# Reordering the factor stage of the first batch: forward factor first, its own banks for the way back, transposes four steps ahead

## Chip, cores, metric

The kernel runs on one core of a Trainium2 chip. The metric is device time in microseconds (us) of one execution; lower is better.

## What is computed

A global filter along the sequence (real FFT, multiplication by a complex filter, inverse real FFT), followed by a feed-forward layer with ELU, all in float32:

```python
# x: (8, 3008, 256); filt_r, filt_i: (1505, 256); w_in: (256, 2048); w_out: (2048, 256)
X = np.fft.rfft(x, axis=1)
Y = X * (filt_r + 1j * filt_i)[None]
y = np.fft.irfft(Y, n=3008, axis=1).astype(np.float32)
h = y.reshape(24064, 256) @ w_in
g = np.where(h > 0, h, np.exp(np.minimum(h, 0)) - 1)
out = g @ w_out
```

The inputs arrive as float64 where the kernel reads the two weights, and it turns their bit patterns into float32 itself.

## The kernel before

**The filter.** The length 3008 is split as 47 times 64. For each of the 8 batches the sequence goes through four matmul stages with tables: a 64-point stage (`a_first` for batch 0, `a_unit` for the others), a 47-point forward factor (`b_unit`), after the multiplication by the filter the 47-point way back (`bi_unit`), and the last 64-point stage (`n_unit`). Between `bi_unit` and `n_unit` the data is turned over through DRAM: `y_write` (L333) stores, `y_read` (L344) loads it in the other order.

The middle stages work on 8 groups, g = 0 to 7 (`NG`). For one group of batch 0:

- `t_first(g)` (L260) transposes with TensorE (PE): eight 112x128 transposes (L269) into two PSUM banks of the pool `psO` (names po0 to po3; group g takes po0 and po1, or po2 and po3, by its parity), which ScalarE (ACT) copies to an SBUF tile t2 in two halves (L270). Tiles of groups 2 and 3 come from the pool `t4p`, all others from `t2p`, two buffers each.
- `b_unit(0, g)` (L299) is the forward factor: four 64x512 products (L297) into two banks, psr and psi. VectorE (DVE) then makes four products with the filter tile ff (L309 to L312): sr, si, and sp, sq (for even g) or the two tiles pq (for odd g). sr and si have two buffers in the pool `sp`.
- `bi_unit(0, g)` (L322) is the way back: eight 64x512 products (L297) from those four tiles into two banks, pva and pvb, which ACT copies to t3 (L329, L330; two buffers).
- `y_write(0, g)` issues two DMAs of 192 KB on SyncE's queue (SP); of the last group one of the two on ACT's.

psr, psi, pva and pvb come from one rotating list of four PSUM banks, `banks` (pool `psM`), so that each pair taken waits for the readers of the pair before the last.

**The weights.** w_in and w_out are read in 16 pieces, k = 0 to 15. `w_fetch(k)` (L546) issues the DMA, `w_split(k)` (L571, DVE, two instructions) masks mantissa and exponent, `w_float(k)` (L579, ACT, four instructions, L584 to L593) makes floats of them, `w_join(k)` (L595, DVE) multiplies them together and for odd k adds the four sums of the fast matrix product (L620 to L623). Even and odd pieces have a set of scratch tiles each. Pieces 7 to 11 are decoded beside the middle stages of batch 0, and pieces 12 to 14 right behind them, as fill work for DVE and ACT.

**The order.** It is written out by hand (`tc.manual_schedule()`): each engine runs its instructions strictly in the order of the program, and semaphores make it wait for what it needs. The order around the change is the loop at L713. It runs ten steps; step g holds group g's forward factor and group g-2's way back, ahead of them the transposes of group g+2 (those of groups 0 to 3 are done before the loop). After the loop come `w_float(12)`, the reading `y_read(0, 0)` (four DMAs of 128 KB, in turn from SP and from ACT), more decoding, the first loads of batch 1, and `n_unit(0, 0)`.

**The main part.** After that a plan mixes the filter stages of batches 1 to 7 into the feed-forward products of the batch before (`up_steps`, `down_steps`, a seven-product scheme for 2x2 blocks), 192 quads in all. This part is not touched.

Of the kernel before, what the change touches and what calls it, by code (L numbers as in the profile page):

```python
# [11 lines left out]
FP32 = mybir.dt.float32  # L12
# [14 lines left out]
P = 128  # L27
D = 256
# [6 lines left out]
NG = K2 // 4  # L35
# [78 lines left out]
def kernel(  # L114
# [25 lines left out]
    t2p = pool("t2p", 2)  # L140
# [3 lines left out]
    t4p = pool("t4p", 2)  # L144
# [4 lines left out]
    psO = pool("psO", 1, space=PSUM)  # L149
# [20 lines left out]
    def bank(name, shape=(P, 2, D)):  # L170
        i = banks.pop(0)
        return i, psM.tile(list(shape), FP32, tag="m%d" % i, name=name)
# [86 lines left out]

    def t_first(g):  # L260

        t = t2s[0, g] = (t4p if g in (2, 3) else t2p).tile([P, 4, D], FP32, tag="t4" if g in (2, 3) else "t2", name="t2")
        for j in range(2):
            i = 2 * (g % 2) + j
            ps = psO.tile([P, 2, 256], FP32, name="po%d" % i)
            for u in range(2):
                k = 4 * g + 2 * j + u
                for dh in range(2):
                    nc.tensor.transpose(ps[0:ROWS, u, ts(dh, P)], zt[k // 16][dh][:, ts(k % 16, ROWS)], eye)  # L269
            nc.scalar.activation(out=t[0:ROWS, 2 * j:2 * j + 2, :], in_=ps[0:ROWS], func=AXT.Copy)  # L270
# [23 lines left out]
    def tile_mm(ps, table, k, rhs, special):  # L294
        for u, w, v in ((0, 1, 1), (1, 1, 0)) if special else ((0, 2, 0),):
            for n, r in enumerate(rhs):
                nc.tensor.matmul(ps[:, u:u + w, :], table[k, v, :], r[k, u:u + w, :], start=n == 0, stop=n == len(rhs) - 1)  # L297

    def b_unit(b, g, f=None, gb=gb, pq=None):  # L299
        t = t2s.pop((b, g))  # L300
        f = fbufs[(b * NG + g) % FBUFS] if f is None else f
        (i0, re), (i1, im) = (bank(n) for n in ("psr", "psi"))
        for o, a in ((0, 0), (64, 2)):
            for ps, k in ((re, LO), (im, HI)):
                tile_mm(ps[o:o + 64], gb, k, [t[:, a:a + 2, :]], g == 0 and a == 0)
        sr, si = (sp.tile([P, 2, D], FP32, tag=n, name=n) for n in ("sr", "si"))
        p, q = pq or (qp.tile([P, 2, D], FP32, tag=n, name=n) for n in ("sp", "sq"))

        nc.vector.tensor_tensor(out=sr, in0=re, in1=f[:, 0], op=ALU.mult)  # L309
        nc.vector.tensor_tensor(out=si, in0=re, in1=f[:, 1], op=ALU.mult)  # L310
        nc.vector.scalar_tensor_tensor(out=p, in0=im, scalar=-1.0, in1=f[:, 1], op0=ALU.mult, op1=ALU.mult)  # L311
        nc.vector.tensor_tensor(out=q, in0=im, in1=f[:, 0], op=ALU.mult)  # L312
        banks.extend((i0, i1))
        if b == 0:

            ss[b, g] = [sr, p], [si, q]
            return
        nc.gpsimd.tensor_tensor(out=sr, in0=sr, in1=p, op=ALU.add)  # L318
        nc.gpsimd.tensor_tensor(out=si, in0=si, in1=q, op=ALU.add)
        ss[b, g] = [sr], [si]  # L320

    def bi_unit(b, g):  # L322
        s = ss.pop((b, g))
        t = t3s[b, g] = t3p.tile([P, 4, D], FP32, tag="t3", name="t3")
        (i0, pa), (i1, pb) = (bank(n) for n in ("pva", "pvb"))
        for o, table, sv in ((0, gr, s[0]), (64, gi, s[1])):
            for ps, k in ((pa, LO), (pb, HI)):
                tile_mm(ps[o:o + 64], table, k, sv, g == 0 and k == LO)
        nc.scalar.activation(out=t[:, 0:2, :], in_=pa, func=AXT.Copy)  # L329
        nc.scalar.activation(out=t[:, 2:4, :], in_=pb, func=AXT.Copy)  # L330
        banks.extend((i0, i1))

    def y_write(b, g, queues=(nc.sync, nc.sync)):  # L333
        if g == 0:
# [236 lines left out]
    def w_split(k):  # L571
        m, e, c = wtmp[k % 2 if k < 15 else 0]
        f, l = c[:, 0], c[:, 1]
        wts[k] = m, e, f, l
        hi = wds[k][:, :, 1]
        nc.vector.tensor_scalar(out=m, in0=hi, scalar1=0x000FFFFF, scalar2=None, op0=ALU.bitwise_and)
        nc.vector.tensor_scalar(out=e, in0=hi, scalar1=0x7FF00000, scalar2=None, op0=ALU.bitwise_and)

    def w_float(k, part=None):  # L579
        m, e, f, l = wts[k]  # L580
        if part == 1:
            return w_power(e)

        nc.scalar.activation(out=l, in_=wds[k][:, :, 0], func=AXT.Identity, scale=2.0 ** -52)  # L584
        nc.scalar.activation(out=f, in_=m, func=AXT.Identity, scale=2.0 ** -20, bias=1.0)
        if part is None:
            w_power(e)
# [56 lines left out]
    with tc.manual_schedule():  # L644


        with tc.tile_pool(name="boot", bufs=1) as bp:
            ff = bp.tile([P, NG, 2, 2, D], FP32, name="ff")
            once = bp.tile([P, 2, P], FP32, name="once")
            eye, gf = once[:, 0], once[:, 1].rearrange("p (v q) -> p v q", v=2)  # L650
            pq = [bp.tile([P, 2, D], FP32, name="pq%d" % i) for i in range(2)]
            zt[0] += [bp.tile([P, 16 * ROWS], FP32, name="zt%d" % i) for i in range(2)]

            for z in zt[0] + zt[1]:
                nc.gpsimd.memset(z.rearrange("p (k r) -> p k r", r=ROWS)[:, :, 48:64], 0.0)
            for k in (1, 2, 3):
                w_fetch(k)
            f_arrange()
            w_fetch(0, nc.sync)
            for c in range(NXC):  # L660
                x_place_first(c)
            for c in range(3):
                x_load_first(c)
            w_fetch(4, nc.sync)
            nc.scalar.memzero(ff[:, 0:NG // 2])
            nc.vector.memset(ff[:, NG // 2:NG], 0.0)
            wtmp.append([kp.tile([P, 512], U32, tag=t, name=n) for t, n in (("k0", "wm"), ("k1", "we"))] +
                        [kp.tile([P, 2, 512], FP32, tag="c", name="wfl")])
            wtmp.append([sdp.tile([P, 2, D], FP32, tag="sd", name=n).bitcast(U32).rearrange("p a b -> p (a b)")
                         for n in ("wm", "we")] +  # L670
                        [t1p.tile([P, XC, D], FP32, tag="t1", name="wfl").rearrange("p (a b) d -> p a (b d)", a=2)])
            for i, v in enumerate((1151.0 * 2 ** 23, 255.0 * 2 ** 23)):
                nc.vector.memset(edges[:, i:i + 1], v)

            def step(k):
                w_split(k)
                w_float(k)
                if k > 0:
                    w_join(k - 1)

            for k in range(3):
                step(k)
            w_fetch(5, nc.sync)
            for c in (3, 4):
                x_load_first(c)
            a_first(0)
            w_fetch(6, nc.sync)
            x_load_first(5)
            nc.sync.dma_start(once, once_d)
            nc.sync.dma_start(gs, gs_d)  # L690
            step(3)
            for c in (1, 2):
                a_first(c)
                w_fetch(c + 6, nc.sync)
            step(4)
            a_first(3)
            w_fetch(9, nc.sync)
            step(5)
            step(6)
            for c in (4, 5):  # L700
                a_first(c)
            tn_read(0, 0)
            for g in range(NG):
                f_read(0, g, ff[:, g])
                if 3 <= g < 5:
                    w_fetch(g + 7)
            for k in (12, 13, 14):
                w_fetch(k)
            w_split(7)
            w_join(6)  # L710
            for g in range(4):
                t_first(g)
            for g in range(NG + 2):  # L713
                if 2 <= g < NG - 2:
                    t_first(g + 2)
                if g >= 2:
                    bi_unit(0, g - 2)
                if g < 5:
                    w_float(g + 7)
                if g < NG:  # L720
                    b_unit(0, g, ff[:, g], gf, pq if g % 2 else None)
                if g >= 2:
                    y_write(0, g - 2, (nc.sync, nc.scalar if g == NG + 1 else nc.sync))
                if g < 4:
                    w_join(g + 7)
                    w_split(g + 8)
                if g == 7:
                    w_join(11)
                    w_split(12)
                    w_split(13)  # L730
            w_float(12)
            y_read(0, 0, (nc.sync, nc.scalar))
            w_float(13)
            w_join(12)
            w_fetch(15)
            w_split(14)
            w_join(13)
            w_float(14)
        for c in range(2):
            x_load(1, c)  # L740
        yp = pool("yp", 2)
# [105 lines left out]
```

## Time and profile before

| | |
|---|---|
| median of 4 runs | 2647.75 us (2646.73 to 2647.93) |
| the profiled execution's own time | 2647.9 us |
| its span, first to last instruction | 2646.1 us |
| granted TensorE clock, mean over the span | 0.993 |
| PE busy, 0 to 44 us | 18.89 us |
| PE busy, 44 to 97 us (the stage of the change) | 41.53 us |
| DVE busy, 44 to 97 us | 39.13 us |
| ACT busy, 44 to 97 us | 32.25 us |
| PE busy, 97 to 120 us | 16.73 us |
| PE busy, 120 to 2646 us | 2517.82 us |

The profile is taken from one execution; its times run from the first instruction. It gives for every instruction its start, duration, source line, and the idle time of its engine just before, with what ended that idle time. "PE" is a matmul, "PEld" the loading of its weights, "SPq" or "ACTq" the issue of a DMA on that engine's queue. A busy PE can run at half speed; the granted clock says so (1.00 is full speed). A float32 matmul shows as several records, and matmuls on different quarters of the array overlap, so that durations of records add up to more than the time that passes.

### The profile page before, as it was taken

How to read it: one execution, taken by the hardware profiler on the slowest of the kernel's cores; microseconds unless marked ns; L12 is line 12 of the kernel's file. 1: busy time of each engine (PE TensorE's matmuls, PEld its weight loads, DVE VectorE, ACT ScalarE, POOL GpSimd, SP SyncE). 2: the span in 40 equal slices, each digit the busy share in tenths (PEclk: the TensorE clock that was granted, in tenths of full speed). 3: DMA queues.
4: the chain of work that ended last, by engine and by line, in shares of the span. 5: the costliest groups of instructions: out<-in, count | busy, mean ns of one | idle time of the engine just before them, and what ended most of it. 6: DMA issues, size and time to landing. Idle time of an engine off the chain costs nothing.

```text
span 2646.1 us, 37334 instructions
## 1 busy us (share of the span) xinstructions
PE 2595.0 (98%) x13508; PEld 2210.0 (84%) x13508; DVE 1843.9 (70%) x3203; ACT 1508.2 (57%) x2622; POOL 237.1 (9%) x298
## 2 busy tenths in 40 slices
PE   5799999999999999999999999999999999999998
PEld 4588789887898878988789878898789887899887
DVE  6777767677676776667767676666767677666766
ACT  6565555555555555655556555565555555555554
POOL 5001100012000210002100020001200011000000
PEclk8899999999999999999999999999999999999999
DMA  9534312523133331423213341134321333110010
GB/s 293 134 95 106 86 38 55 126 73 84 39 97 87 80 78 43 103 69 101 72 31 98 85 113 49 39 90 107 98 50 41 79 81 82 38 41 19 21 29 17
DMA packets 224456, 202.85 MB, mean 77 GB/s; under 512 B 127586, under 2 KB 191090, under 8 KB 224272
## 3 DMA queue, kind: packets, MB, share of 16 engines
q1 hardware_dynamic: 211632, 166.70, 25.0%
q0 software_dynamic: 11184, 33.04, 4.8%
q8 instruction: 107, 1.75, 0.3%
q10 hardware_dynamic: 1456, 0.72, 0.1%
q14 instruction: 77, 0.63, 0.1%
HBM read 128.52 MB, written 74.97 MB: 77 GB/s over the span
## 4 chain that ended last, share of the span: by engine, by line
PE 96%; DMA 2%; DVE 1%; POOL 0%; issue 0%; ACT 0%; DVEq 0%; SPq 0%; POOLq 0%; ACTq 0%
PE po L490 43%; PE phs L408 25%; PE phd L408 12%; PE pha L408 6%; PE psn L360 3%; PE pva L297 2%; PE psr L297 2%; PE psa L209 2%; DMA fd<-in_filt_i_dram 1%; DMA ff<-fd 0%; DMA wd<-in_moe_w_out_dram 0%; DMA fd<-in_filt_r_dram 0%; PE pvb L297 0%; DMA yd<-t 0%; PE psi L297 0%
## 5 line engine op out<-in xcount | busy, mean ns | idle before, releaser
L490 PE MATMUL po<-g,wo 128*128 128x256 f32 (+1 forms) x5376 | 1296.7, 375 | 0.0
L490 PEld LDWEIGHTS po<-g,wo 128*128 128x128 f32 x5376 | 1015.0, 190 | 129.5 <-issue 15.8
L419 ACT ACTIVATE g<-phs 128x512 f32<-128x512 f32 (+1 forms) x576 | 338.9, 588 | 842.8 <-PE phs L408 842.2
L416 DVE TENSOR_TENSOR g<-phd,g 128x512 f32<-128x512 f32 (+1 forms) x384 | 259.6, 676 | 457.2 <-ACT e L426 282.3
L426 ACT ACTIVATE e<-e 128x512 f32<-128x512 f32 (+1 forms) x768 | 477.1, 621 | 24.4
L408 PE MATMUL phs<-y,wi 128*128 128x256 f32 (+1 forms) x1536 | 394.8, 379 | 0.0
L408 PE MATMUL phs<-ys,wi 128*128 128x256 f32 (+1 forms) x1536 | 387.6, 375 | 0.7 <-ACT g L419 0.6
L430 DVE SCALAR_TENSOR_TENSOR g<-e,g 128x512 f32<-128x512 f32 (+1 forms) x576 | 387.2, 672 | 0.0
L425 ACT ACTIVATE e<-g 128x512 f32<-128x512 f32 (+1 forms) x576 | 353.0, 613 | 32.6 <-DVE g L416 27.4
L408 PEld LDWEIGHTS phs<-y,wi 128*128 128x128 f32 x1536 | 284.5, 190 | 83.1 <-ACT t L329 34.1
L408 PEld LDWEIGHTS phs<-ys,wi 128*128 128x128 f32 x1536 | 291.4, 190 | 34.5 <-ACT g L419 1.4
L430 DVE SCALAR_TENSOR_TENSOR g<-e,phs 128x512 f32<-128x512 f32 (+1 forms) x192 | 130.0, 677 | 136.9 <-ACT e L426 136.7
L408 PE MATMUL phd<-ys,wi 128*128 128x256 f32 (+1 forms) x768 | 194.1, 375 | 1.2 <-DVE g L416 1.2
L408 PE MATMUL pha<-y,wi 128*128 128x256 f32 (+1 forms) x768 | 193.8, 375 | 0.0
L408 PE MATMUL phd<-y,wi 128*128 128x256 f32 (+1 forms) x768 | 193.7, 375 | 0.0
L425 ACT ACTIVATE e<-phs 128x512 f32<-128x512 f32 (+1 forms) x192 | 113.0, 588 | 141.4 <-PE phs L408 140.5
L318 POOL TENSOR_TENSOR sr<-sr,sp 128x512 f32<-128x512 f32 x56 | 71.1, 1270 | 1246.6 <-DVE sp L311 1246.6
L408 PEld LDWEIGHTS phd<-ys,wi 128*128 128x128 f32 x768 | 145.5, 190 | 18.6 <-DVE g L416 2.3
L408 PEld LDWEIGHTS pha<-y,wi 128*128 128x128 f32 x768 | 145.8, 190 | 16.8 <-ACT y L362 0.2
L408 PEld LDWEIGHTS phd<-y,wi 128*128 128x128 f32 x768 | 145.8, 190 | 16.5
L467 DVE TENSOR_TENSOR g<-g,g 128x512 f32<-128x512 f32 (+1 forms) x192 | 130.7, 681 | 6.7
L470 DVE TENSOR_TENSOR g<-g,g 128x512 f32<-128x512 f32 (+1 forms) x192 | 130.7, 681 | 6.6
(133 smaller groups left out, 2372.0 us busy)
## 6 DMA issues: line engine op xcount, KB each, us to landing
yd<-t SPq DMA_DIRECT2D x127, 192.0 KB
t<-yd SPq DMA_DIRECT2D x190, 128.0 KB
z<-t SPq DMA_DIRECT2D x84, 256.0 KB
f<-fd POOLq DMA_DIRECT2D x112, 192.0 KB, 3.6
t<-z SPq DMA_DIRECT2D x224, 96.0 KB
out_dram<-o SPq DMA_DIRECT2D x632, 32.0 KB
tn<-tn_t SPq DMA_DIRECT2D x48, 256.0 KB
xc<-in_x_dram SPq DMA_DIRECT2D x84, 128.0 KB
```

The lines of the kernel that those rows point to most:

```text
L297: nc.tensor.matmul(ps[:, u:u + w, :], table[k, v, :], r[k, u:u + w, :], start=n == 0, stop=n == len(rhs) - 1)
L318: nc.gpsimd.tensor_tensor(out=sr, in0=sr, in1=p, op=ALU.add)
L360: nc.tensor.matmul(ps[:, ts(q, P)], t[:, i - 4 * m, ds(dh * P, P)], w[:, i - 4 * m, :], start=True, stop=True)
L408: nc.tensor.matmul(ps[:, a, 0:h], w_in[q][:, COMBO[n], a, :], y[n], start=start and a == 0, stop=True, skip_group_check=True)
L416: nc.vector.tensor_tensor(out=g[o], in0=i0, in1=i1, op=ALU.add)
L419: nc.scalar.activation(out=g[o], in_=i0, func=AXT.Copy)
L425: nc.scalar.activation(out=e, in_=src, func=AXT.Relu, scale=-1.0)
L426: nc.scalar.activation(out=e, in_=e, func=AXT.Exp, scale=-1.0)
L430: nc.vector.scalar_tensor_tensor(out=g[n], in0=es[n], scalar=1.0, in1=src, op0=ALU.subtract, op1=ALU.max)
L467: nc.vector.tensor_tensor(out=b12, in0=b22, in1=b12, op=ALU.subtract)
L470: nc.vector.tensor_tensor(out=g["t4"], in0=g["b21"], in1=g["t2"], op=ALU.subtract)
L490: nc.tensor.matmul(po[i][:, u, 0:h], w_out[q][:, COMBO[n], a, :], g[n][:, a, :], start=q == 0 and a == 0 and n in (1, 3, 6, 4), stop=True, ...
```

## The change

The change touches the first batch's middle stages alone.

- In each step the forward factor's products of group g come first, then the way back of group g-2 (called between those products and the four multiplies, through the new argument `between`), then the transposes of group g+4. Before, the order was transposes of g+2, way back, forward factor.
- The rotating list of four banks is left to the forward factor. The way back of batch 0 takes its banks from `psO`: po2 and po3 for groups 0 to 2, then po0 and po1 for odd and po2 and po3 for even groups.
- Transposes of groups 4 to 7 all go through po0 and po1. Their SBUF tiles are taken from `t4p` for groups 2, 3, 6 and 7.
- Fill work: `w_float(g+7)` now follows the transposes in step g. `w_join` and `w_split` run in steps 0 to 2 instead of 0 to 3; piece 11 is split in step 2, and piece 10 is joined in step 7, ahead of piece 11. After the loop `w_float(14)` stands before `w_join(13)`, which leaves the order on each engine as it was.

```diff
     def t_first(g):
-        t = t2s[0, g] = (t4p if g in (2, 3) else t2p).tile([P, 4, D], FP32, tag="t4" if g in (2, 3) else "t2", name="t2")
+        pool, tag = (t4p, "t4") if g % 4 > 1 else (t2p, "t2")
+        t = t2s[0, g] = pool.tile([P, 4, D], FP32, tag=tag, name="t2")
         for j in range(2):
-            i = 2 * (g % 2) + j
-            ps = psO.tile([P, 2, 256], FP32, name="po%d" % i)
+            i = j + 2 * (g % 2 if g < 4 else 0)
+            ps = psO.tile([P, 2, 256], FP32, tag="po%d" % i, name="po%d" % i)
...
-    def b_unit(b, g, f=None, gb=gb, pq=None):
+    def b_unit(b, g, f=None, gb=gb, pq=None, between=None):
...
                 tile_mm(ps[o:o + 64], gb, k, [t[:, a:a + 2, :]], g == 0 and a == 0)
+        if between:
+            between()
...
     def bi_unit(b, g):
...
-        (i0, pa), (i1, pb) = (bank(n) for n in ("pva", "pvb"))
+        if b == 0:
+            pa, pb = (psO.tile([P, 2, 256], FP32, tag="po%d" % i, name="po%d" % i)
+                      for i in ((0, 1) if g > 2 and g % 2 else (2, 3)))
+        else:
+            (i0, pa), (i1, pb) = (bank(n) for n in ("pva", "pvb"))
...
-        banks.extend((i0, i1))
+        if b > 0:
+            banks.extend((i0, i1))
...
             for g in range(NG + 2):
-                if 2 <= g < NG - 2:
-                    t_first(g + 2)
-                if g >= 2:
-                    bi_unit(0, g - 2)
+                back = (lambda g=g: bi_unit(0, g - 2)) if g >= 2 else None
+                if g < NG:
+                    b_unit(0, g, ff[:, g], gf, pq if g % 2 else None, back)
+                else:
+                    back()
+                if g < 4:
+                    t_first(g + 4)
                 if g < 5:
                     w_float(g + 7)
-                if g < NG:
-                    b_unit(0, g, ff[:, g], gf, pq if g % 2 else None)
+                if g < 3:
+                    w_join(g + 7)
+                    w_split(g + 8)
+                if g == 2:
+                    w_split(11)
                 if g >= 2:
                     y_write(0, g - 2, (nc.sync, nc.scalar if g == NG + 1 else nc.sync))
-                if g < 4:
-                    w_join(g + 7)
-                    w_split(g + 8)
                 if g == 7:
+                    w_join(10)
                     w_join(11)
                     w_split(12)
                     w_split(13)
...
             w_split(14)
+            w_float(14)
             w_join(13)
-            w_float(14)
```

## The prediction

> **What bounds the kernel now.** I read the page first, its second part: TensorE (PE) is saturated from about 116 us to the end, and only the first two of the 40 slices have room.
>
> ```profile
> span 2646.1 us, 37334 instructions
> PE   5799999999999999999999999999999999999998
> PEclk8899999999999999999999999999999999999999
> ```
>
> So whatever this change gains or loses must show as a shift of the moment at which that saturated stretch begins. The chain of work that ended last, in order of time around 93 us, names what precedes it:
>
> ```profile
> 93.86 3.07 DMA yd<-t
> ...
> 97.51 3.63 DMA t<-yd
> ...
> 101.38 3.54 PE psn L360 x16
> ```
>
> The last way back of batch 0 is evicted, written to DRAM, read back transposed, and then feeds the first real product (psn). Every microsecond by which 96.9 (issue of the reading) moves, moves the rest. What fills 49 to 94 us the table of waits and the DVE (VectorE) timeline tell:
>
> ```profile
> DVE sr L309 <- PE psi L297: 12.1, 4, 5.4
> ACT t L329 <- PE pvb L297: 7.8, 4, 3.0
> ```
>
> ```profile
> 75.71 0.68 DVE L312 TENSOR_TENSOR sq<-psi,ff 128x512 f32<-128x512 f32 x1
> 77.65 0.69 DVE L309 TENSOR_TENSOR sr<-psr,ff 128x512 f32<-128x512 f32 x1 [1.26 <-PE psi L297]
> ...
> 84.34 0.69 DVE L309 TENSOR_TENSOR sr<-psr,ff 128x512 f32<-128x512 f32 x1 [4.21 <-PE psi L297]
> ...
> 88.09 0.69 DVE L309 TENSOR_TENSOR sr<-psr,ff 128x512 f32<-128x512 f32 x1 [1.26 <-PE psi L297]
> ```
>
> Columns: start, us, what, idle before it. Up to 76.4 DVE is busy without a gap (multiplies and weight decoding in turn); afterwards it waits for the forward factor. Two things make it wait. The ScalarE (ACT) evictions of transposes 6 and 7 stand until forward 4 and 5 have ended and hold the way-back evictions behind them, and PE runs at half clock after its own gaps:
>
> ```profile
> 72.63 1.08 ACT L270 ACTIVATE t<-po 112x512 f32<-112x512 f32 x2 [2.00 <-PE psi L297]
> 77.69 1.08 ACT L270 ACTIVATE t<-po 112x512 f32<-112x512 f32 x2 [0.55 <-PE psi L297]
> ```
>
> ```profile
> 80.00:82.00 2.00, 2.00 (x16) 1.04 (x14) 0.14 (x1) 0.00 (x0) 0.00 (x0) 0.67 0.63 152
> 82.00:84.00 2.00, 2.00 (x12) 0.70 (x6) 0.00 (x0) 1.08 (x2) 0.00 (x0) 0.50 0.13 45
> ```
>
> (Busy time by stretch; the third figure from the right is the granted clock.)
>
> **Prices.** F = forward factor, W = way back, T = transposes of one group, M = its four multiplies. From the PE timeline at full clock: F 65.08 to 66.05, 1.0 (1.05 behind a wait: 71.48 to 72.55); W 67.06 to 69.03, 2.0 to 2.1 (I use 2.06; W0 with its extra pieces 52.95 to 55.82, 2.9); T 66.05 to 67.06, 1.0. DVE starts: M 50.29 to 52.69, 2.4; join 7 52.69 to 56.40, 3.7; join 8 59.47 to 61.40, 1.9; join 9 64.55 to 68.18, 3.6; join 10 71.25 to 73.24, 2.0; a split 0.67. ACT: two evictions 1.0 (58.76 to 59.71); one float 2.5 (49.93 to 52.44).
>
> **The walk after the change.**
> - T4 now stands before float 7 on ACT: F0 ends at 50.2, T4 51.2, its evictions 50.7 to 51.7, float 7 to 54.2. Join 7 started at 52.69 and now at 54.25: **1.6 lost**, on DVE, which sets the end here.
> - DVE from there: join 7 57.9, split 8 58.6, M1 61.0, join 8 62.9, split 9 63.6, M2 66.0, join 9 69.6, splits 10 and 11 70.9, M3 73.3, M4 75.7 (before 76.3). Join 10 (2.0) has left this stretch, hence the 0.6 gained despite the lost 1.6. PE is ahead all this time (F2, W0, T6 by 58.1; F3, W1, T7 by 66; F4, W2 by 69.3), so the three DVE-bound steps cost nothing on PE. Floats 8 and 9 end 0.8 before their joins; that cover is thin, and what exceeds it adds one for one. T5 to T7 through two banks instead of four wait at most for an eviction of 0.5, behind which PE has slack.
> - F5 needs M3 (four banks: the unit two before), so 73.3 + 0.15 = 73.5. PE stood nearly idle from 69.3. In this trace the clock was halved from 60.1 to 63.5 and from 80.7 to 84.1, 3.4 each (two-microsecond rows), each after a stretch with PE busy half the time or less; 67.0 to 70.4, busy about 60%, was followed by full clock. So I take one cold stretch of 3.4 there: F5 and W3 (3.1 of work) end at 78.1 instead of 76.5, **about 1.6 lost**.
> - PE then sets the pace: F6 79.1, W4 81.2, F7 82.2, W5 84.3, W6 86.3, W7 88.4, evictions 89.4. Before: 93.84. M(g) rewrites tiles that W(g-2) reads (two buffers each). Before, W(g-2) stood ahead of F(g), so this never waited; now it follows, and M(g) ends about 1.4 after W(g-2) (si starts some 0.4 before W ends, then three multiplies of 0.6). M7 thus ends at 85.7 (before 90.5), and F first buys no more overlap than that. The freed t2 buffers remove the two ACT waits shown above; the way-back banks, two pairs in turn, are free two steps before.
> - **What is late next.** Two of the reading's four DMAs are issued by ACT behind float 12, and that stands behind split 12, join 11 and now join 10 too. Before:
>
> ```profile
> 96.14 0.72 ACT L593 ACTIVATE we<-we,edges 128x512 uint32<-128x512 f32 x1
> 96.90 0.80 ACTq L347 DMA_DIRECT2D t<-yd  x2
> ```
>
> From M7's end: 2.0 (join 10) + 3.7 (join 11) + 0.35 (first op of split 12) + 1.95 (last three ops of float 12, 94.86 to 96.86 less queueing) = 8.0, so 93.7. The last y_write lands at 89.5 + 3.1 = 92.6. The decoding takes the place of the write as the last wait, and gives back 1.1 of the gain.
> - The reading: 96.9 to 93.7, **3.2 gained**. SP's half goes out 1 us earlier, then x loads follow it on SP, beside ACT's half. This overlap is in no row of before. Ends: its half alone could land 0.9 sooner (half of 3.63 hidden, less issue); in a saturated stretch the ff DMAs took 6.3 to 8.3, so up to 2.7 later at their fastest. I take 0.2 later, near the row of the same transfer. Floats 13 and 14 (5.1 from 94.1) let go of ACT at 99.2, as the first half of psn ends; joins 12 and 13 move with float 12. So **3.0** carries to 116 us and, PE being full there, to the end.
>
> Sum: the profiled execution's own 2647.9 (span 2646.1 and 1.8 around it) less 3.0 = 2644.9; the median of the four runs, 2647.75, is 0.15 lower, hence 2644.8. Not known within this: the place of the cold stretches (1.7 either way), the semaphore hops (0.5), the reading (0.9 sooner to 2.7 later).
>
> [...] The row: PE ran only transposes from 44.0 to 49.1, and the granted clock rose from 0.50 through 0.87 to 1.00 there.
>
> ```profile
> 44.00:46.00 2.00, 1.65 (x9) 1.26 (x8) 0.90 (x3) 0.98 (x3) 1.59 (x4) 0.50 1.03 225
> 46.00:48.00 2.00, 2.00 (x18) 2.00 (x17) 0.00 (x0) 1.74 (x4) 0.00 (x0) 0.87 1.07 236
> 48.00:50.00 2.00, 2.00 (x23) 1.63 (x25) 0.00 (x0) 2.00 (x6) 1.35 (x3) 1.00 1.04 225
> ```
>
> [...]
>
> **Rivals.**
> - *Warm tail.* F5 and W3 find full clock (1.6), and psn, cold for all of its 3.54 before (1.78 at 125.05), is cold for half of it only (0.9): gain 5.5, 2642.3. [...] Against: PE idle from 69.3 to 73.5, longer than the gap of 56 to 58.5 that was followed by half clock.
> - *Collision on DMA.* ACT's half of the reading, now behind x loads, takes the 6.3 of the saturated row: 2.7 of the gain gone, 2647.5. For: DMA share 0.97 to 1.07 from 98 to 104. Against: the same x loads followed on its heels before.
> - *The decoding turns it slower.* The place is ACT's issue behind float 12, the price 2.0 for join 10 on a chain of 8.0 from M7; it decides once M7 ends after 88.8, 3.1 later than in my walk. If M and W wait for each other in turn (M(g) for W(g-2), F(g+2) for M(g)), PE has gaps in each step and the three stretches from 77 to 88 go cold too, 1.7 each: M7 at 90.8, reading at 98.8, 1.9 slower: 2649.8, and up to 2655 if psn's own chain is cold as well. Against: in the walk M6 ends 1.8 before W6 needs it, so PE has no gap.
>
> **Numbers.** Forecast 0.58, warm tail 0.20, collision 0.13, slower 0.09. Less than 0.2% (5.3 us) of this kernel cannot be told from no change: faster needs under 2642.5, most of the warm tail and a little of the forecast, 0.18; slower needs over 2653.0, part of the last rival, 0.06; within 0.76. The range that leaves out 2 in 10: 2641.5 (a warm tail) to 2649.5 (collision, and the near end of the last rival); the forecast's own is 2642.8 to 2646.8.
>
> **What would show it.** In the new profile: join 7 starting near 54.3 behind ACT; DVE without gaps from there to M4 at about 75.7; M5 to M7 waiting for PE's way back, not for F; W7 evicted near 89.4; ACT's reading issued near 93.7, right after float 12 and later than the last write lands; psn some 3 us before 101.4. Wrong if DVE still waits for F in the tail, if half clock returns after 77 us, or if psn starts much later than 3.8 us after ACT's issue.

## The result and the profile after

| | before | after |
|---|---|---|
| median, us | 2647.08 (53 runs) | 2643.94 (33 runs) |
| ratio, 95% interval | 1 | 0.9988 [0.9983, 0.9993] |
| profiled execution: own time / span | 2647.9 / 2646.1 | 2643.35 / 2641.5 |
| first multiply M0 starts | 50.29 | 50.50 |
| M7 ends | 90.57 | 83.99 |
| psn starts (lasts) | 101.38 (3.54) | 95.94 (3.75) |
| first psa of batch 1 | 118.46 | 113.46 |

The change gains 3.1 us in the median, 0.12%: real by its interval, and inside the 0.2% that the prediction calls no change. The forecast was 2644.8. The two profiled executions lie 4.6 apart, because the one of before was 0.8 above its median and the one of after 0.6 below; places are read from these two, the size of the gain from the medians.

The page of after, the two that answer to the first ones shown of before:

```profile
span 2641.5 us, 37322 instructions
...
PE   5899999999999999999999999999999999999998
```

TensorE still fills every slice but the first two. The chain that ended last, around the hand-over (start, us, what):

```profile
88.02 3.51 DMA yd<-t
...
92.21 3.49 DMA t<-yd
...
95.94 3.75 PE psn L369 x16
```

It has the same links as before, 5.4 sooner at psn: last write to DRAM, reading, first product. DVE (start, us, what, idle before):

```profile
54.69 0.69 DVE L608 SCALAR_TENSOR_TENSOR we<-wd,we 128x512 uint32<-128x512 uint32 x1 [1.70 <-ACT we L602]
...
75.68 0.69 DVE L315 TENSOR_TENSOR sq<-psi,ff 128x512 f32<-128x512 f32 x1
76.28 0.69 DVE L312 TENSOR_TENSOR sr<-psr,ff 128x512 f32<-128x512 f32 x1
...
78.76 0.68 DVE L312 TENSOR_TENSOR sr<-psr,ff 128x512 f32<-128x512 f32 x1
...
81.33 0.68 DVE L312 TENSOR_TENSOR sr<-psr,ff 128x512 f32<-128x512 f32 x1
```

Join 7 waits 1.70 for float 7. After that no wait stands on any multiply: the three of 1.26, 4.21 and 1.26 ahead of M5, M6 and M7 are gone. M5, M6 and M7 start 2.4 to 2.6 apart. Two lines of the table of waits, from 49 to 97 us (us in total, times, longest), name what is new:

```profile
DVE we L608 <- ACT we L602: 2.8, 2, 1.7
...
ACT t L337 <- DMA yd<-t: 2.6, 2, 2.1
```

The rows of before, DVE on psi with 12.1 and ACT on pvb with 7.8, have shrunk to 5.1 (only the start, ahead of M0) and 5.0. The second line here was not there before: evictions of the way back standing for a DMA. It is seen on ACT at the end of the stretch:

```profile
85.27 0.60 ACT L337 ACTIVATE t<-po 128x512 f32<-128x512 f32 x1 [2.07 <-DMA yd<-t]
...
86.91 0.60 ACT L337 ACTIVATE t<-po 128x512 f32<-128x512 f32 x1 [0.55 <-DMA yd<-t]
...
88.02 0.38 ACTq L347 DMA_DIRECT2D yd<-t  x1
...
91.35 0.72 ACT L602 ACTIVATE we<-we,edges 128x512 uint32<-128x512 f32 x1
91.60 0.80 ACTq L356 DMA_DIRECT2D t<-yd  x2
```

The results of the way back lie in two t3 buffers, so W6's eviction needs y_write(4) to have landed, and W7's needs y_write(5). Before, the groups came slowly enough for that never to show. The last two lines show the other late thing: float 12's last operation began only 0.25 ahead of ACT's half of the reading, and SP's half left at 91.72. The write and the decoding end together.

**The sum.** From M0's start to M7's end I subtract DVE's own waits that the rows show (0.2 and more; M0's start is not counted). What is left is work:

| kernel | M0 to M7's end | DVE waits in it | rest | M7's end to psn | psn to psa |
|---|---|---|---|---|---|
| before | 40.28 | 6.73 | 33.55 | 10.81 | 17.08 |
| after | 33.49 | 1.70 | 31.79 | 11.95 | 17.52 |

From profile to profile psa of batch 1 (the first product of the next batch) thus moves by 0.21 (M0) - 6.73 (waits for the forward factor) + 1.70 (join 7) - 1.76 (join 10 moved out; its own row is 2.0) + 1.14 (M7 to psn) + 0.44 (psn to psa) = -5.00, which is 118.46 to 113.46. In the span 4.6 are left.

Where psa starts decides the time: in the twelve kernels of this study the profiled execution's own time less psa's start lies between 2529.1 and 2529.9. And one part of it no edit here touches: up to M0 the program of all twelve is the same, yet M0 starts between 47.93 us (e6) and 53.66 us (e11). Places are therefore counted from M0 below.

### The profile page after: what moved, and what is told of

Same layout as the page of the kernel before. It is cut to its first block, busy times and chain, and to the rows that moved or that the text cites. A ratio compares the mean times of both kernels' runs of the same rounds, so it can differ in the third digit from the quotient of the medians.

```text
span 2641.5 us, 37322 instructions
## 1 busy us (share of the span) xinstructions
PE 2594.0 (98%) x13508; PEld 2212.1 (84%) x13508; DVE 1843.4 (70%) x3203; ACT 1508.3 (57%) x2622; POOL 236.9 (9%) x298
## 4 chain that ended last, share of the span: by engine, by line
PE 96%; DMA 2%; DVE 1%; ACT 0%; issue 0%; SPq 0%; DVEq 0%; POOL 0%; ACTq 0%
PE po L499 43%; PE phs L417 25%; PE phd L417 12%; PE pha L417 6%; PE psn L369 3%; PE pva L298 2%; PE psr L298 2%; PE psa L209 2%; DMA xc<-in_x_dram 1%; DMA x<-in_x_dram 0%; DMA f<-in_moe_w_out_dram 0%; DMA yd<-t 0%; PE po L298 0%; PE po L270 0%; PE pvb L298 0%; PE psi L298 0%
## 5 line engine op out<-in xcount | busy, mean ns | idle before, releaser
L321 POOL TENSOR_TENSOR sr<-sr,sp 128x512 f32<-128x512 f32 x56 | 71.2, 1271 | 1246.3 <-DVE sp L314 1246.3
```

## The experiments

My theory after the result: the gain comes from buffers (t2 tiles and banks of their own) and from join 10, not from the forward factor's place; what limits it now is a chain of near ties (join 7, the clock, t3, the decoding). Rivals: the forward factor's order does it; or one of the near ties hides several us that could be had. The table has them as above (M0 to M7's end, DVE's waits in it, the rest):

| kernel | median, us | ratio to before | M0 to M7's end | DVE waits | rest | M7 to psn | psn to psa |
|---|---|---|---|---|---|---|---|
| e1 tiles only | 2644.79 | 0.9991 [0.9982, 1.0] | 37.26 | 3.78 | 33.48 | 10.49 | 17.29 |
| e2 back first | 2643.44 | 0.9986 [0.9977, 0.9995] | 32.22 | 0.47 | 31.75 | 11.43 | 17.30 |
| e3 shared banks | 2658.36 | 1.0047 [1.0035, 1.006] | 48.83 | 16.42 | 32.41 | 11.77 | 17.29 |
| e4 join 10 back | 2642.94 | 0.9985 [0.9976, 0.9994] | 35.47 | 1.80 | 33.67 | 11.45 | 17.53 |
| e5 float 7 first | 2642.73 | 0.9983 [0.9974, 0.9992] | 34.55 | 2.72 | 31.83 | 11.99 | 17.43 |
| e6 four t3 | 2642.57 | 0.9982 [0.9973, 0.9991] | 34.84 | 2.93 | 31.91 | 11.72 | 17.38 |
| e7 warm psn | 2643.81 | 0.9987 [0.9978, 0.9996] | 33.61 | 1.90 | 31.71 | 11.78 | 16.47 |
| e9 = e5+e6+e7 | 2641.24 | 0.9977 [0.9968, 0.9986] | 34.45 | 2.72 | 31.73 | 11.60 | 16.65 |
| e10 = e2+e5+e6+e7 | 2641.14 | 0.9975 [0.9966, 0.9984] | 34.71 | 3.12 | 31.59 | 12.14 | 16.10 |
| e11 = e9, reading on SP | 2641.35 | 0.998 [0.9971, 0.9989] | 32.25 | 0.52 | 31.73 | 11.92 | 16.32 |

The column "rest" carries most of this study: with join 10 inside the stretch it is 33.5 to 33.7 (before, e1, e4), without it 31.6 to 31.9 in every kernel but e3, whose shorter waits I did not subtract. All else is waits, by the way that the column is formed, and these differ.

### e1: only the tiles

Before, with T6 and T7 in the free tiles of another pool; order, banks and decoding as before.

```
-        t = t2s[0, g] = (t4p if g in (2, 3) else t2p).tile(...)
+        pool, tag = (t4p, "t4") if g % 4 > 1 else (t2p, "t2")
+        t = t2s[0, g] = pool.tile([P, 4, D], FP32, tag=tag, name="t2")
```

> The kernel before with one part of the change: the tiles of transposes 6 and 7 from the other pool, so that their evictions no longer stand on ScalarE until forward 4 and 5 have ended. My theory shares the gain out: this part lets the way-back evictions 2 to 4 go 1 to 2 us earlier and brings the first psn about 2 us forward, some 2645 against 2647 before. Rival (all of the gain comes from the order and the banks): within 0.5 us of before, and VectorE's waits for the forward factor stay at 12 us.

psn follows M0 by 47.75 instead of 51.09, 3.3 sooner, and the median is 2.2 below before. So by the medians two thirds of the gain come from one line (e1's interval reaches 1.0, so the share is rough). What it leaves, on its DVE:

```profile
77.37 0.69 DVE L310 TENSOR_TENSOR sr<-psr,ff 128x512 f32<-128x512 f32 x1 [1.26 <-PE psi L298]
...
81.11 0.69 DVE L310 TENSOR_TENSOR sr<-psr,ff 128x512 f32<-128x512 f32 x1 [1.26 <-PE psi L298]
...
84.86 0.69 DVE L310 TENSOR_TENSOR sr<-psr,ff 128x512 f32<-128x512 f32 x1 [1.26 <-PE psi L298]
```

The wait of 4.21 has become 1.26: the tiles took away ACT's wait behind the forward factor, and this tail ran at full clock, where before it was halved from 80.7 to 84.1; the row does not tell the two apart. A regular 1.26 per group stays, with groups 3.74 apart. TensorE shows why:

```profile
80.00 0.61 PE L298 MATMUL psi<-t,once 48*64 48x512 f32 x1 [0.15 <-DVE pq L313]
```

F6's products for psi stand until M5's last multiply (end 79.85) has read the bank, and M6 starts 1.11 after them. This loop of F and M takes 2.48 + 0.15 + 1.11 = 3.74; the way back, done before, is not in it. Before's M5 and M7 waited for the same 1.26.

### e2: way back ahead of the forward factor

After, with the order of products inside a step as before; tiles, banks and decoding as after.

```
+        if between:
+            between()
         t = t2s.pop((b, g))
...
                 tile_mm(ps[o:o + 64], gb, k, [t[:, a:a + 2, :]], g == 0 and a == 0)
-        if between:
-            between()
```

> The changed kernel with one part undone: in each step the way back's products stand ahead of the forward factor's. My theory: in the tail both must run once per step anyway, VectorE sets the pace, and the order inside the step is worth at most 1 us of psn's start (some 2644 to 2645). Rival (forward first is the source of the gain): each multiply group of the tail waits about 2 us for the way back ahead of its forward factor, psn's start falls back by 4 us or more, and the time stands at about that of before, 2647.

The waits of 1.26 do not come back: DVE waits 0.47 in all, and the median is 0.5 below after's, its ratio inside after's interval. Forward first, the part of the change named first, is worth nothing that can be measured here; nor is it between e9 and e10 below (2641.24 and 2641.14). What removed the 1.26 are then most likely the banks of F's own, since the loop of e1 runs through the shared bank. The banks added to e1 alone were not run; the other parts left are the transposes four steps ahead and the fill work, of which e4 puts join 10 back without the 1.26.

### e3: no banks of its own for the way back

After, with pa and pb of batch 0 taken from the rotating list as before.

```
-        if b == 0:
+        if False:
...
-        if b > 0:
-            banks.extend((i0, i1))
+        banks.extend((i0, i1))
```

> The changed kernel with one part undone: the way back takes its two banks from the rotating list again, so that the forward factor is left with two banks of the four. My theory: forward g+1 must wait until multiply group g has ended, and VectorE shows the gap of 1.26 us of before again ahead of each of the groups 4 to 7; psn 4 to 5 us later than with the change, 2648 to 2649. Rival (TensorE paces the tail, banks do not matter): within 1 us of the changed kernel, 2644.

Far more than I expected: 14.4 us over after, and 11.3 over before.

```profile
71.03 0.69 DVE L607 SCALAR_TENSOR_TENSOR we<-wd,we 128x512 uint32<-128x512 uint32 x1 [4.26 <-ACT we L601]
...
80.95 0.69 DVE L312 TENSOR_TENSOR sr<-psr,ff 128x512 f32<-128x512 f32 x1 [2.44 <-PE pva L298]
...
88.21 0.69 DVE L312 TENSOR_TENSOR sr<-psr,ff 128x512 f32<-128x512 f32 x1 [3.98 <-PE pva L298]
```

With F ahead and the banks shared, the way back W(g-2) needs the banks that M(g-1) still reads, and M(g) must not rewrite the products that W(g-2) still reads (the wait on pva). Floats on ACT queue behind the late evictions, so join 9 waits 4.26, and TensorE stays at half clock from 57 to 74 and 78 to 88 us. The new order needs the new banks; without them it is the slowest kernel of this study. My expected figure had only a wait of the forward factor for the multiplies in it, 1.26 per group.

### e4: join 10 back in the stretch

```
-                if g < 3:
+                if g < 4:
                     w_join(g + 7)
                     w_split(g + 8)
-                if g == 2:
-                    w_split(11)
...
-                    w_join(10)
```

> The changed kernel with the fill work of before: piece 10 is joined in step 3 and piece 11 split there, no longer ahead of piece 11 at the end. My theory: VectorE has no gap up to the last multiplies, so they end 2.0 us later, and with them the last write; the reading stands behind that write, not behind float 12, so nothing is given back: psn 2 us later, 2646. Rival (the decoding chain behind the last multiplies was the last wait): psn's start does not move, 2644.

The work returns in full: the rest is 33.67, 1.9 above after. From M0 to psn the profile has 46.92, 1.5 over after's 45.44. The median does not show it: 2642.94, 1.0 below after, where it should have been above (the intervals overlap). In this run half clock lay from 70.9 to 77.7 and cost a wait of only 0.25, since the join kept DVE busy while TensorE caught up; at the same place it costs 1.9 to 3.1 in the kernels below that have no join there. That is a reading of the trace and not a test of it. As a test of time this run decided nothing.

### e5: float 7 ahead of the transposes of group 4

```
+                if g == 0:
+                    w_float(7)
                 if g < 4:
                     t_first(g + 4)
-                if g < 5:
+                if 0 < g < 5:
                     w_float(g + 7)
```

> The changed kernel with one edit: in step 0 float 7 stands ahead of the evictions of transposes 4 on ScalarE. My theory: the join of piece 7 no longer waits 1.7 us, and as VectorE runs without a gap from there to the last multiplies, the whole chain comes 1.5 us earlier: first psn 43.9 us after the first multiplies instead of 45.4, time 1.5 us below the changed kernel's. Rival (TensorE or the writes pace the tail): the wait moves to the tail and psn comes at 45.4 again.

The wait of join 7 is gone, but this execution does not show that the edit removed it. M0 stood for its ff load up to 49.73, and join 7 started at 52.13. In after float 7 ends 4.28 behind T4's first transpose (50.38 to 54.66); in e5 that transpose starts at 47.64, so that with after's order float 7 would have ended at 51.9, early enough too. e7, without the edit, has no such wait either. M7 is no sooner after M0 (34.55; after 33.49), and psn comes 46.54 after M0, not 43.9. That a wait moves to the tail, the rival's first half, is what the profile shows: DVE waits 1.70 and 0.79 in M5 and 0.23 ahead of M6, on the way back. TensorE had stood idle for M3 before, and then ran at half clock from 70.5 to 77.3, where F5 and W3 stand:

```profile
70.22 1.74 PE L298 MATMUL psr<-t,once 48*64 48x512 f32 x2 [3.33 <-DVE si L313]
```

```profile
75.45 0.69 DVE L312 TENSOR_TENSOR sr<-psr,ff 128x512 f32<-128x512 f32 x1 [1.70 <-PE po L298]
```

```profile
72.00:74.00 2.00, 2.00 (x12) 0.97 (x8) 1.75 (x3) 1.36 (x3) 0.00 (x0) 0.50 0.69 178
```

(The third figure from the right is the granted clock.)

### e6: four result buffers

W6 and W7 of batch 0 write into free x tiles.

```
-        t = t3s[b, g] = t3p.tile([P, 4, D], FP32, tag="t3", name="t3")
+        if b == 0 and g > 5:
+            t = xp.tile([P, 2, 2, D], FP32, tag="xc", name="xc").rearrange("p k u d -> p (k u) d")
+        else:
+            t = t3p.tile([P, 4, D], FP32, tag="t3", name="t3")
```

> The changed kernel with one edit: the way back of groups 6 and 7 goes to free tiles of another pool, so that its evictions need not wait for the writes of groups 4 and 5. My theory: the last eviction comes 0.9 us earlier and the last write too, but the reading's half on ScalarE stands behind float 12, which is done only 0.2 us before the write lands now; psn moves by 0.3 us or less. Rival (the write alone is the last wait): psn 0.9 us earlier.

The waits of 2.07 and 0.55 are gone: the last eviction ends at 85.39, 2.6 after M7 (4.0 in after). psn follows M7 by 11.72 instead of 11.95. On ACT:

```profile
85.42 0.40 ACTq L351 DMA_DIRECT2D yd<-xc  x1
...
90.13 0.72 ACT L606 ACTIVATE we<-we,edges 128x512 uint32<-128x512 f32 x1
90.29 0.80 ACTq L360 DMA_DIRECT2D t<-yd  x2
```

The reading stands behind float 12 now, 7.5 after M7. The two late things were a tie, and taking away one is worth 0.2. The median is 1.4 below after's, more than that, but the intervals overlap.

### e7: unused products keep the clock up for psn

Ten products of 128x512, whose results nobody reads, between W7 and psn.

```
+            warm = psO.tile([P, 2, 256], FP32, tag="po2", name="po2")
+            for i in range(10):
+                nc.tensor.matmul(warm, eye, ff[:, 0, 0], start=True, stop=True)
```

> The changed kernel with ten products of 128x512 added, whose result nobody uses, on TensorE between the last way back and the first psn, so that it does not stand idle for 10 us. My theory: psn runs at full clock, 1.8 instead of 3.75 us, but VectorE's join of piece 13 ends at 98.8 us and takes its place: 1.4 us of it carry to the saturated part. Rivals: all of it carries (2.6 us, with the half clock behind psn); or none, if float 14 and join 13 hold the evictions.

```profile
85.19 8.85 PE L746 MATMUL po<-ff,once 128*128 128x512 f32 x20
94.99 2.02 PE L369 MATMUL psn<-tn,t 128*128 128x128 f32 x16 [0.95 <-DMA t<-yd]
```

psn takes 2.02 instead of 3.75, and 1.05 of these 1.7 is still there at psa. The weight decoding takes the rest: ACT takes up the first half of psn at 96.46, as float 14 lets go of it, and DVE starts on the result (ys) at 98.05, as join 13 ends. The median, 0.1 below after's, does not show the gain.

### e9, e10, e11: the edits together

e9 is e5, e6 and e7 in one kernel; e10 has e2's order besides; e11 is e9 with this:

```
-            y_read(0, 0, (nc.sync, nc.scalar))
+            y_read(0, 0)
```

> The three edits of the other kernels together on the changed kernel: float 7 first, free tiles for the way back of groups 6 and 7, ten unused products ahead of psn. My theory: 1.5 (VectorE's chain) plus 0.3 plus 1.4, some 3 us below the changed kernel, 2640.5. Rival (one wait only takes the place of the other): within 1 us of the best of the three alone.

> The changed kernel with four edits together: the way back's products ahead of the forward factor's in each step, float 7 ahead of the transposes of group 4, the results of the last two ways back in free x tiles, and the ten unused products ahead of psn. The back-first run alone started psn 43.65 us after the first multiply, and the ten products brought psa 16.47 after psn instead of 17.52. Theory (the order of the two factors costs nothing, and once the writes no longer hold the evictions, float 12 of the weight decoding is the last wait): M7 ends 32 us after the first multiply as in the back-first run, float 12 lets ACT's half of the reading go 8.0 later and psn follows 3.9 after that, at 44.0; psa at 60.5 after the first multiply, 2.5 sooner than in the changed kernel (63.0), so about 2641.5 us. Rival (where the half-clock stretch falls decides, as in the run with three of these edits): psn 46.0 after the first multiply, psa 62.6, 2643.5 us. Second rival (forward first does matter once the other waits are gone): DVE waits of over 1 us on the forward factor return ahead of M5 to M7, psn at 46 or later, with the waits on psi.

> The run with float 7 first, x tiles for the last two ways back and ten unused products, and besides all four DMAs of the reading issued by SP, none by ACT behind float 12. In that run SP's half went out at 91.64 and ACT's at 92.59, 46.05 us from the first multiply to psn. Theory (the decoding is the last wait there, by 0.95): SP needs some 0.4 per DMA, so its third and fourth leave at 92.4 and 92.8 where ACT's two left at 92.6 and 93.0; psn comes 0.2 sooner at most, 45.8, and x loads behind it on SP 0.8 later; time the same within 0.5, 2641 us. Rival (ACT's late half is what psn waits for, and its transfer starts when the queue is free): psn 0.9 sooner, 45.1, time 2640.3. Second rival (four DMAs in one queue, with x loads no longer beside them, land one after the other): psn 1 later.

All three lie within 0.2 us of each other, 2641.1 to 2641.4, some 2.7 below after and 5.4 to 6.4 below the runs of before beside them. They beat both kernels by the medians; against after the intervals still touch (0.9966 to 0.9984 for e10, 0.9983 to 0.9993 for after). The profiles do not show where the 2.7 come from: from M0 to psa e9 has 62.70 and e10 62.95, against after's 62.96, since waits of 2.72 and 3.12 stand in M5 and M6; only e11 has less, 60.49. The sum expected for e9 (1.5 + 0.3 + 1.4) is thus not shown, though its median, 2641.24, is 0.7 from it. For e10 the rival with the half clock came nearest (psn 46.0, psa 62.6 after M0; measured 46.85 and 62.95): psn was not at 44.0, with waits of 2.51 ahead of M5 and 0.61 ahead of M6:

```profile
76.46 0.69 DVE L312 TENSOR_TENSOR sr<-psr,ff 128x512 f32<-128x512 f32 x1 [2.51 <-PE psr L298]
```

They are on the forward factor, as the second rival had it, since it stands behind the way back in this kernel. But e5 and e9, forward first, wait as long there on the way back, so I put them down to the clock again; the stretches of e10 (third figure from the right is the granted clock, the second column PE's busy time and count):

```profile
66.00:68.00 2.00, 1.34 (x14) 0.19 (x5) 1.90 (x6) 0.02 (x1) 0.00 (x0) 1.00 1.03 414
68.00:70.00 2.00, 0.08 (x1) 0.11 (x2) 2.00 (x6) 1.76 (x3) 0.00 (x0) 1.00 0.67 242
70.00:72.00 2.00, 2.00 (x9) 0.73 (x13) 2.00 (x4) 2.00 (x5) 0.00 (x0) 0.62 0.02 8
```

TensorE idles while DVE decodes, and the half clock arrives just as the products do that DVE waits for. In e11, which up to the reading is the code of e9, it fell elsewhere:

```profile
56.00:58.00 2.00, 1.95 (x14) 1.00 (x14) 1.97 (x5) 0.00 (x0) 1.74 (x4) 0.50 0.95 223
...
70.00:72.00 2.00, 2.00 (x11) 1.35 (x8) 1.90 (x5) 1.21 (x3) 0.00 (x0) 0.50 0.27 98
```

Half clock from 56 to 73 us, and DVE waited 0.52 in all, none of it in the tail: in the earlier steps DVE sets the pace, and the tail ran at full clock. psn came 44.17 after M0, though M0 itself was late (53.66, behind an ff load). What e11 was made for, whether ACT's late half of the reading holds psn, it did not settle: its last write took 4.42 to land, so the reading left at 93.36, 7.45 after M7, the same as behind float 12.

## Why the prediction was right, and where it was not

The median was 0.9 below the forecast, and the mechanism was mostly as forecast. Two terms between M4 and M7 were priced too high, both in the same direction: 10.0 us predicted from M4's end to M7's, 7.62 measured. In the profiled pair psn came 5.4 sooner and not 3.0. That the medians lie 3.1 apart, so near to the 3.0, is therefore luck in part.

- **Join 7 behind float 7**: predicted 54.3 and 1.6 lost, measured 54.69 and 1.70. Right in this execution, but no constant: e7, with the same code there, shows no such wait (float 7 ends at 51.2, M0 at 52.1, so join 7 can start), and e2 0.47. It depends on how long M0 stands for its ff load while the transposes go on: in e7 M0 started 2.6 after F0's last product, in after as soon as it had ended.
- **DVE without a gap up to M4 (75.7)**: right; M4 ended at 76.37, and join 7's start makes 0.4 of the difference.
- **The t2 tiles and banks remove the waits on F**: right, 6.73. In e1 the tiles, with the clock's help, take 2.95 of them (6.73 to 3.78), and in after, with the banks, the rest is gone. The loop through the shared bank, 1.26 per group, was missing from the "two things" that make DVE wait. "F first buys no more overlap" was right too (e2).
- **One cold stretch of 3.4 at 70, costing 1.6**: read from a single trace, and not there in after. Half clock lay from 60.4 to 70.6, where DVE sets the pace, and cost no DVE wait. The sign that I went by failed too: PE was busy 2.08 of the 3.4 us before it (61%), hardly less than the 2.15 from 67.0 to 70.4 in before that were followed by full clock. In five variants (e5, e6, e7, e9, e10) a stretch lay near the predicted place, from about 68 to 78, but was twice as long and cost 1.9 to 2.7 in four and 3.1 in e10. So the place held in some kernels and the length in none of these.
- **TensorE's pace of 3.1 per step**: the term that was mis-sized. I added F's 1.0 and W's 2.06, each taken from its own first start to its last end, 3.06 in all. The records of F and W overlap where one follows the other on the array: F6 and F7 start 2.57 apart.

```profile
75.82 0.59 PE L298 MATMUL psr<-t,once 48*64 48x512 f32 x1
...
78.39 0.59 PE L298 MATMUL psr<-t,once 48*64 48x512 f32 x1
```

  Records on one part of the array follow at 0.43 here (psr at 75.82 and 76.25, po of the way back at 76.68, 77.11, 77.54 and 77.97), and six of these (two of F, four of W) make a step. From M4's end to M7's are three steps of 2.54, hardly more than the 2.4 that M takes by itself; with 3.1 and the 1.6 I had M7 end at 85.7, and it was 83.99. My fear that M(g) waits for W(g-2) came to 0.1 to 0.2 per group.
- **The decoding takes the write's place as the last wait, at M7 + 8.0**: near. ACT's half of the reading left at M7 + 7.61, and behind float 12 in e6, e9 and e10 at 7.5. But in after the write was last still, by 0.1 or so, for a reason that I had not seen: the two t3 buffers, 2.6 of waits. The give-back of 1.1 came out as 1.14 all the same, by luck: from M7's end to the issue of the last write it took 4.03 instead of 3.29 (t3), the write 3.51 instead of 3.07 to land, and the decoding only tied with it.
- **The reading 3.2 sooner, psn 3.0**: 5.3 and 5.4 in the profile: M7 was 1.7 sooner than in the walk and the reading 0.4 sooner after M7, and psn followed ACT's issue by 4.34 instead of 4.48. psn to psa then returned 0.44: psn ran at half clock as before, and the half clock went on for 1.6 behind it (up to 101.3).
- **3.0 at the end**: 3.1 in the medians, 4.6 in the profiled pair. The forecast's size agrees with the medians, while its walk (2644.9) ends 1.6 after the one profiled (2643.35). Since only one execution of each kernel is profiled, how the median's 3.1 divides is not shown; that executions differ by where M0 and the half clock fall is what the variants suggest, not what a second profile of after has shown.
- **The rivals**: the warm tail did occur in this execution (products at full clock from 71 us), its other half, a warm psn, did not. The collision on DMA did not: psn came 4.34 after ACT's issue, before 4.48. M and W in turn, the slower case, is e3's picture, with the shared banks; with banks of its own M waits 0.1 to 0.2.
- **Transposes and the clock**: the row shown in the prediction came again. In after too TensorE ran only transposes from 45.0 to 49.3, and the granted clock went 0.50, 0.82, 1.00 in the rows from 44 to 50 (before 0.50, 0.87, 1.00).

## What to carry to other kernels

Split a stretch into the pacing engine's own work and its waits before pricing an edit: here the work was the same to 0.3 us in eleven of the twelve kernels but for one moved join, and every other difference was a wait, or the place of M0. A change of order and a change of buffers that come together are to be tried apart; here the buffers gave the gain, and the new order without the new banks cost 11 us. A gain upstream of near ties is worth the distance to the next late thing only, so list every buffer count on the way (t3 was missing from my list), and take the pace of back-to-back products from start to start of the same product, not from the sum of two durations.

## What the runs showed of the hardware

- The half-clock stretches that begin between 55 and 80 us, worked out from the granted clock of the two-microsecond rows, last about 3.4, 6.8, 10.2 or 17.0 us: 60.1 to 63.5 before, 70.5 to 77.3 in e5 and in e10, 60.4 to 70.6 in after, 55.9 to 72.9 in e11. The longer ones are about two, three and five times the 3.4 of before. e9 and e11, the same code up to the reading, met the half clock at different places (71.2 to 78.0 and 55.9 to 72.9). I had counted on one stretch of 3.4, and mostly it lasted twice that or more.
- In e11 the clock stayed halved for 17 us although TensorE's busy time reads 1.9 to 2.0 of each 2.0; these rows hold only 5 to 17 records, against 24 in after's rows from 76 to 82, at full clock. The count alone does not tell when a cold stretch ends either: before's rows from 80 to 84 hold 16 and 12, and full clock was back at 84.1; after's from 62 to 66 hold 13 each, and the clock stayed halved up to 70.6. What brings it back is open here.
- Ten unused 128x512 products (8.85 us at 85 to 94, e7) kept the clock at 1.00 up to psn and made psn 2.02 instead of 3.75.
- y_write is not of fixed length: the last write landed after 3.07 in before, 3.51 in after and 4.42 in e11, a spread as large as what most edits here could gain.
